# The last product of a chained matrix kernel, made in two PSUM banks and added to a kept copy of its chain

## The chip, the cores and the metric

The kernel runs on one core of one Trainium2 chip. The metric is the device time of one execution in microseconds (us). Most of it is the span, from the first to the last instruction that the profile shows; the time is some 1.8 us longer than the span.

In the lines of the profile, PE is the tensor engine, ACT is ScalarE, DVE is VectorE and SP is SyncE; a q behind the name is the engine's sequencer, which issues stores. L562 is a line of the kernel, x16 a number of instructions. A row in order of time begins with start and duration in us, and its bracket gives the idle time of the engine before it and what ended that.

## The reference, cut to what matters

Linformer attention (8 batches, 8 heads, 1024 tokens, 64 channels per head, keys and values projected to 64 rows) gives x with 8192 rows of 512. Then comes a feed-forward layer with a squared relu:

```python
def _moe_ref(x, w_in, w_out) -> np.ndarray:
    h = np.maximum(x @ w_in, 0.0)          # 8192 x 2048
    return (h * h @ w_out).astype(np.float32)   # 8192 x 512
```

## The kernel before: the parts that matter

The kernel works in chunks of 512 tokens. Both matrix products of the feed-forward layer are done with seven block products in place of eight (a Strassen-Winograd scheme). In the second one, a block product is 16 matmuls of 128x256: 8 for each half of the rows. Four output blocks come out of it. PSUM is the memory that the tensor engine writes, and a bank of it holds one block product here: half 0 and half 1 of its rows stand side by side, 256 columns each. Products 1, 6, 7 and 4 are a **chain**: they add up one after the other in one PSUM bank, and between them what has been added so far is copied or stored. The last output block, `put(1, 0, ...)`, is the whole chain, with product 4 on top.

```python
def keep(self, ps):                        # a copy of a bank in SBUF
    u = part_pool.tile([P, DM], F32, name="u")
    nc.scalar.copy(u[:], ps)
    return u

def put(self, a, mh, ps, more=None, part=None):
    o = out_pool.tile([P, 2, HM], F32, name="o_sb")
    n = slice(0, 2) if part is None else slice(part, part + 1)
    ps = ps.rearrange("p (i m) -> p i m", i=2)[:, n]
    if part:
        nc.vector.tensor_copy(o[:, n], ps)
    elif more is None:
        nc.scalar.copy(o[:, n], ps)
    else:
        tt(o[:, n], ps, ALU.add, more.rearrange("p (i m) -> p i m", i=2)[:, n])
    i = 4 * self.c + a + 2 * n.start
    (nc.scalar if part == 0 else nc.sync).dma_start(...)      # cut

def second_seven(self, first, chain, other, last=False):
    ...                                    # cut: products 1, 5, 6, 2
    yield from product(7, chain)
    self.put(1, 1, chain, p5)
    yield
    yield from product(3, other)
    self.put(0, 1, other, u2)
    yield
    yield from product(4, chain)
    if last:                               # the last chunk of all
        self.put(1, 0, chain, part=0)      # ScalarE copies half 0, its queue stores it
        self.put(1, 0, chain, part=1)      # VectorE copies half 1, SyncE stores it
    else:
        self.put(1, 0, chain)
    yield
```

At the start of the kernel, while the first loads are on their way, `warm(n)` runs n matmuls of zeros, meant to bring the tensor engine to full clock: in the trace of the kernel before, the first 8 of them start every 0.43 us and the next four every 0.22. The first call is `warm(8)`.

The softmax here doesn't subtract the row's maximum and nothing guards it: scores larger than these inputs give would overflow.

## Time and profile before

| | kernel before |
|---|---|
| time, median of the first 3 runs | 474.89 us (473.21 to 474.94) |
| span of the profiled run | 471.5 us |
| tensor engine busy | 98% of the span |
| end of the last matmul in the chain of waits | 467.81 us |
| end of the last instruction that computes | 468.70 us |
| from the start of the last matmul (467.53) to the end of the span | 3.94 us |

The last row is what I call **the tail** from here on. It starts at a record of the trace and not at a modelled end. To read it: the tensor engine bounds the kernel up to 467.8 us, so whatever a change does elsewhere shows only if it moves the last matmul or what follows it.

### The profile page before, as it was taken

The numbers are of one execution on the slowest core, as the hardware profiler recorded it, in microseconds if no ns is written. First come the engines' busy times: TensorE is split into PE (matmuls) and PEld (weight loads), VectorE is DVE, ScalarE is ACT, GpSimd is POOL, SyncE is SP. The second block draws the span as 40 slices with busy tenths as digits, with TensorE's granted clock in tenths as the row PEclk, the third lists the DMA queues.
The fourth block names the chain that finished last, engine by engine and source line by source line (L and its number), as shares of the span: only waits on it lengthen the run. The fifth ranks groups of instructions, "written<-read, shape, count | busy, mean of one in ns | idle before, by whom it ended". The sixth has DMA issues, their size and how long they took to land.

```text
span 471.5 us, 10107 instructions
## 1 busy us (share of the span) xinstructions
PE 464.1 (98%) x4123; PEld 367.6 (78%) x4141; DVE 347.6 (74%) x595; ACT 297.5 (63%) x484; POOL 34.0 (7%) x47
## 2 busy tenths in 40 slices
PE   8999999999999999999999999999999999999996
PEld 4544677888788787887888888888878878888885
DVE  2469985776968779567895779787796679968571
ACT  4488585887467864677457774568636875555641
POOL 7430100100010000100001000100000000000000
PEclk9999999999999999999999999999999999999999
DMA  9999999895869578785969749695692154101012
GB/s 182 201 205 207 158 206 203 166 217 106 186 138 207 137 141 195 133 171 131 170 180 153 170 98 183 153 197 147 116 219 71 39 132 100 68 24 68 24 69 89
DMA packets 85743, 67.90 MB, mean 144 GB/s; under 512 B 34368, under 2 KB 82240, under 8 KB 85696
## 3 DMA queue, kind: packets, MB, share of 16 engines
q0 software_dynamic: 32208, 29.23, 40.6%
q1 hardware_dynamic: 53344, 37.89, 30.1%
q8 instruction: 32, 0.52, 0.4%
q10 hardware_dynamic: 144, 0.13, 0.1%
q14 instruction: 15, 0.12, 0.1%
HBM read 59.24 MB, written 16.78 MB: 161 GB/s over the span
## 4 chain that ended last, share of the span: by engine, by line
PE 97%; DMA 1%; DVE 1%; ACT 1%; issue 0%; SPq 0%; ACTq 0%; DVEq 0%
PE ps_bank L665 38%; PE ps_second L585 36%; PE ps_bank L502 6%; PE ps_bank L562 3%; PE ps_att L270 3%; PE ps_att L339 2%; PE ps_second L562 2%; PE ps_att L415 2%; DMA k_f<-in_k_dram 1%; PE ps_att L392 1%; PE ps_bank L314 1%; PE ps_att L349 1%; PE ps_att L345 1%; PE ps_bank L220 0%; PE ps_att L289 0%; PE ps_bank L278 0%
## 5 line engine op out<-in xcount | busy, mean ns | idle before, releaser
L154 DVE TENSOR_TENSOR h<-h 128x1024 bf16<-128x1024 bf16 (+1 forms) x170 | 105.4, 645 | 43.9 <-ACT h L675 38.7
L665 PE MATMUL ps_bank<-x_sum,w_in_sum 128*128 128x256 bf16 x672 | 101.1, 273 | 0.1
L665 PEld LDWEIGHTS <-w_in_sum 128*128 128x128 bf16 x896 | 85.5, 98 | 18.9 <-issue 6.3
L585 PEld LDWEIGHTS <-h 128*128 128x128 bf16 x896 | 87.6, 98 | 10.7
L679 DVE CUSTOM_DVE_ANT_0 h<-ps_bank,u 128x512 bf16<-128x512 f32 x112 | 73.8, 685 | 16.2 <-PE ps_bank L665 12.1
L557 ACT COPY u<-ps_bank 128x512 f32<-128x512 f32 x115 | 68.0, 591 | 24.9 <-PE ps_bank L665 23.7
L690 ACT COPY ps_bank<-ps_bank 128x512 f32<-128x512 f32 x56 | 32.0, 571 | 81.5 <-PE ps_bank L665 81.5
L675 ACT ACTIVATE h<-ps_bank 128x512 bf16<-128x512 f32 x112 | 67.9, 607 | 16.7 <-PE ps_bank L665 15.8
L665 PEld LDWEIGHTS <-w_in 128*128 128x128 bf16 x672 | 64.3, 98 | 14.5 <-issue 5.2
L585 PEld LDWEIGHTS <-s 128*128 128x128 bf16 x672 | 65.7, 98 | 7.6
L665 PE MATMUL ps_bank<-xT,w_in 128*128 128x256 bf16 x448 | 67.3, 273 | 0.3
L585 PE MATMUL ps_second<-w_out_sum,s 128*128 128x256 bf16 x448 | 67.2, 273 | 0.0
L585 PE MATMUL ps_second<-w_out_sum,h 128*128 128x256 bf16 x448 | 67.0, 273 | 0.0
L585 PE MATMUL ps_second<-w_out,h 128*128 128x256 bf16 x448 | 64.7, 272 | 0.0
L419 DVE TENSOR_TENSOR xT<-ps_att,rs 128x512 bf16<-128x512 f32 x48 | 30.9, 685 | 13.7 <-PE ps_att L415 13.7
L353 ACT ACTIVATE expT<-ps_att 128x1024 bf16<-128x1024 f32 x32 | 33.1, 1034 | 5.2 <-PE ps_att L339 3.4
L665 PE MATMUL ps_bank<-x_sum,w_in 128*128 128x256 bf16 x224 | 33.7, 273 | 0.3
L665 PE MATMUL ps_bank<-xT,w_in_sum 128*128 128x256 bf16 x224 | 33.6, 273 | 0.1
L154 DVE TENSOR_TENSOR o_sb<-ps_second,u 128x512 f32<-128x512 f32 x29 | 19.9, 685 | 18.7 <-PE ps_second L585 13.6
L585 PE MATMUL ps_second<-w_out,s 128*128 128x256 bf16 x224 | 33.6, 273 | 0.0
L502 PE MATMUL ps_bank<-xT,w_in 128*128 128x512 bf16 x124 | 28.8, 379 | 0.4 <-issue 0.2
L154 DVE TENSOR_TENSOR s<-h 128x1024 bf16<-128x1024 bf16 x32 | 22.0, 691 | 3.7 <-PE ps_second L585 3.0
(97 smaller groups left out, 453.4 us busy)
## 6 DMA issues: line engine op xcount, KB each, us to landing
out_dram<-o_sb SPq DMA_DIRECT2D x63, 256.0 KB, 2.5
rs<-inv SPq DMA_DIRECT2D x96, 128.0 KB, 2.3
K_sb<-in_k_dram POOLq DMA_DIRECT2D x7, 1024.0 KB, 10.2
V_sb<-in_v_dram POOLq DMA_DIRECT2D x7, 1024.0 KB, 14.5
Q_sb<-in_q_dram POOLq DMA_DIRECT2D x6, 1024.0 KB, 11.8
w_out<-in_moe_w_out_dram POOLq DMA_DIRECT2D x4, 512.0 KB, 15.8
Q_sb<-in_q_dram POOLq DMA_DIRECT2D x4, 256.0 KB, 11.0
V_sb<-in_v_dram POOLq DMA_DIRECT2D x2, 512.0 KB, 10.8
```

The lines of the kernel that those rows point to most:

```text
L154: return nc.vector.tensor_tensor(out=o, in0=x, in1=y, op=op)
L270: nc.tensor.matmul(ps[LO, 0], lhsT=ET[:, i, :], rhs=self.K[:, :, i, :], start=f, stop=l)
L353: self.done = nc.scalar.activation(e[:], ps[:], AF.Exp, scale=SCALE)
L419: self.done = nc.vector.tensor_tensor(out=self.xT[:, pr, :, par], in0=ps_x[par].rearrange("p (c t) -> p c t", c=2), in1=rs[:, par].rearran ...
L502: nc.tensor.matmul(ps[:], lhsT=w_in_blk(cb, fb), rhs=self.xT[:, cb, self.c].rearrange("p a t -> p (a t)"), start=(cb == 0), stop=(cb == NC ...
L557: nc.scalar.copy(u[:], ps)
L562: nc.tensor.matmul(ps[:, i * HM:(i + 1) * HM], lhsT=self.h_form(n, fb)[:, i * P:(i + 1) * P], rhs=w_out_form(n, fb), start=fresh and i == ...
L585: nc.tensor.matmul(ps[:, i * HM:(i + 1) * HM], lhsT=self.h_form(n, fb)[:, i * P:(i + 1) * P], rhs=w_out_form(n, fb), start=fresh and i == ...
L665: nc.tensor.matmul(ps[:, j * HC:(j + 1) * HC], lhsT=w_in_form(n, cb, 2 * self.g + j), rhs=self.chunk.x_form(n, cb), start=fresh and j == 0 ...
L675: nc.scalar.activation(self.out(kh, a), ps[:], AF.Relu)
L679: nc.vector._custom_dve(TENSOR_ADD_SAT, out=self.out(kh, a), in0=ps[:], in1=more[:], s0=3.0e38, s1=0.0)
L690: nc.scalar.copy(self.chain[:], self.first[:])
```

## The change

The intent is to let the first half of the last block be finished and stored while the tensor engine makes the second half. In the kernel before, two engines work in one bank only in turn (VectorE's copy starts only at 468.28 us, when ScalarE's is done, though they read different columns), so each half gets a bank of its own. A fresh bank does not hold the chain, so the chain is copied to SBUF after product 7 (`u3`) and added by VectorE when a half is stored. The core of the diff, cut at the lines of dots:

```diff
-        def put(self, a, mh, ps, more=None, part=None):
-            o = out_pool.tile([P, 2, HM], F32, name="o_sb")
+        def put(self, a, mh, ps, more=None, part=None, o=None):
+            o = out_pool.tile([P, 2, HM], F32, name="o_sb") if o is None else o
...
-            if part:
-                nc.vector.tensor_copy(o[:, n], ps)
-            elif more is None:
+            if more is None:
                 nc.scalar.copy(o[:, n], ps)
...
-            (nc.scalar if part == 0 else nc.sync).dma_start(
+            nc.sync.dma_start(
...
             yield from product(7, chain)
+            if ends:
+                u3 = self.keep(chain)
             self.put(1, 1, chain, p5)
...
-            yield from product(4, chain)
-            if last:
-                self.put(1, 0, chain, part=0)
-                self.put(1, 0, chain, part=1)
+            if ends:
+                o = out_pool.tile([P, 2, HM], F32, name="o_sb")
+                for i, ps in enumerate(ends):
+                    self.half_product(4, i, ps, True)
+                    self.put(1, 0, ps, u3, i, o)
+                    yield
             else:
+                yield from product(4, chain)
                 self.put(1, 0, chain)
...
-        run(chunk[B - 1, 1].second_seven(..., True))
+        run(chunk[B - 1, 1].second_seven(..., [bank(n=turn["bank"] + n)[:] for n in (2, 3)]))
```

More of the change, by code (lines that the diff above doesn't have):

```diff
@@ L563, in half_product @@
                     ps[:, i * HM:(i + 1) * HM], lhsT=self.h_form(n, fb)[:, i * P:(i + 1) * P],
-                    rhs=w_out_form(n, fb), start=fresh and i == 0 and fb == 0, stop=fb == HF - 1,
+                    rhs=w_out_form(n, fb), start=fresh and fb == 0, stop=fb == HF - 1,
                     skip_group_check=True,
                 )
-        def put(self, a, mh, ps, more=None, part=None):
-            o = out_pool.tile([P, 2, HM], F32, name="o_sb")
+        def put(self, a, mh, ps, more=None, part=None, o=None):
+            o = out_pool.tile([P, 2, HM], F32, name="o_sb") if o is None else o
             n = slice(0, 2) if part is None else slice(part, part + 1)
             ps = ps.rearrange("p (i m) -> p i m", i=2)[:, n]
-            if part:
-                nc.vector.tensor_copy(o[:, n], ps)
-            elif more is None:
+            if more is None:
                 nc.scalar.copy(o[:, n], ps)
@@ L622, in second_spread, with second_seven @@
             yield
-        def second_seven(self, first, chain, other, last=False):
+        def second_seven(self, first, chain, other, ends=None):
             def product(n, ps, fresh=False):
@@ L627, in product @@
                 yield
-                self.half_product(n, 1, ps, fresh)
+                self.half_product(n, 1, ps)
             yield from product(1, first, True)
@@ L647, in second_seven @@
             yield
-            yield from product(4, chain)
-            if last:
-                self.put(1, 0, chain, part=0)
-                self.put(1, 0, chain, part=1)
+            if ends:
[4 more added lines that the diff above has]
+                    yield
             else:
+                yield from product(4, chain)
                 self.put(1, 0, chain)
-            yield
+                yield
     class Group:
@@ L900 @@
         assert not plan, plan
-        run(chunk[B - 1, 1].second_seven(second_bank(0)[:], second_bank(1)[:], bank(n=turn["bank"] + 1)[:], True))
+        run(chunk[B - 1, 1].second_seven(second_bank(0)[:], second_bank(1)[:], bank(n=turn["bank"] + 1)[:], [bank(n=turn["bank"] + n)[:] for n in (2, 3)]))
 _INS = ['q', 'k', 'v', 'E', 'F', 'moe_w_in', 'moe_w_out']
```

## The prediction

> **What bounds the kernel now.** I read the page first, then the chain that ended last over the last microseconds, then the instructions in order of time there, then the movement of the DMA engines in the last 3.5 us. The page says who owns the 471.5 us span:
>
> ```profile
> PE 464.1 (98%) x4123; PEld 367.6 (78%) x4141; DVE 347.6 (74%) x595; ACT 297.5 (63%) x484; POOL 34.0 (7%) x47
> ...
> PE 97%; DMA 1%; DVE 1%; ACT 1%; issue 0%; SPq 0%; ACTq 0%; DVEq 0%
> ```
>
> The tensor engine is busy for 98% of the span and is 97% of the chain; the clock row of the page is 9 in all 40 slices, so no throttle confuses this. A change that neither removes nor shortens matmuls can only touch the ends, where the tensor engine is not the bound. The change sits at the very end, so I looked at the chain from 463 us on (start, duration, what):
>
> ```profile
> 466.05 1.76 PE ps_second L562 x16
> 467.81 0.03 ACTq L575
> 467.84 0.04 issue
> 467.88 0.38 ACT o_sb L575
> 468.26 0.02 issue
> 468.28 0.42 DVE o_sb L573
> ```
>
> The last product is 16 matmuls from 466.05 to 467.81. Then ScalarE copies one half of the rows out of the bank, and only when it is done does VectorE copy the other half: **the two engines work one after the other although they were meant to share the work.** The same in order of time, with what ended each engine's idle time in brackets:
>
> ```profile
> 467.88 0.37 ACT L575 COPY o_sb<-ps_second 128x256 f32<-128x256 f32 x1 [4.70 <-PE ps_second L562]
> 468.28 0.38 ACTq L579 DMA_DIRECT2D out_dram<-o_sb  x1
> 468.28 0.42 DVE L573 COPY o_sb<-ps_second 128x256 f32<-128x256 f32 x1 [1.50 <-ACT o_sb L575]
> ```
>
> The bracket of the last line names ScalarE as the releaser. And ScalarE's copy of the first half began after the 16th matmul, though the matmuls of its own half, the first 8 of 16, must have been done at about 466.05 + 1.76/2 = 466.93. Both are one cause: everything that touches one bank is put in sequence by bank.
>
> After 468.70 only the last store is left. In the last 3.5 us, in slices of 0.0875 us:
>
> ```profile
> DMA  9999610000000499955999510000000000000000
> ```
>
> The two bursts are the two 128 KB stores: the first from about 469.15 to 469.55, the second from about 469.6 to 470.05. Each begins some 0.9 us after its issue (468.28 and 468.70); they stand side by side and hardly overlap. The profile puts landing 1.8 us after issue, 470.5, and the program ends 1.0 us later.
>
> [...] the trace has 691 and 692 ns for the adds into o_sb. [...] this trace has no fp32 add of 256. [...] here a 128 KB store takes 1.8 us and a 256 KB one 2.1, so halving a store hardly shortens its landing.
>
> **The change part by part.** Between the two programs the orders of instructions, with line numbers taken out, are the same on VectorE, ScalarE, GpSimd and SyncE up to the last few rows; on the tensor engine 16 products go to other banks. So the first 462 us should not change at all.
>
> *Kept copy (added).* Product 7 leaves the chain in a bank at 464.30. ScalarE now copies it to SBUF, 128x512 fp32, 586 ns by the same copy at other places: about 464.37 to 464.96. ScalarE has been idle since 463.19, so it costs ScalarE nothing. But the add of the same bank into o_sb on VectorE, which began at 464.40 and took 0.69, now must wait for ScalarE: about 464.98 to 465.67. Its next add waits for the tensor engine until 466.09 anyway: 0.4 us to spare. Hidden.
>
> *Two fresh banks (moved).* Half 0 (8 matmuls) ends at 466.93, half 1 at 467.81 as before: 16 matmuls of the same form and the same weights. The first matmul of product 4 had to wait for VectorE to leave the chain; that wait was already over (465.09 against 466.05), so nothing is won there. Starting a bank afresh in place of adding is a flag of the matmul and costs nothing that I can see in the other fresh products (0.0 us idle ahead of them). The banks were last used by the first stage, before 455 us.
>
> *Half 0 stored early (moved off the path).* VectorE is busy with the previous add until 466.78, so its add of half 0 is about 466.97 to 467.40, its issue on SyncE 467.40 to 467.77. SyncE had its earlier issue done at 466.81 + 0.37 = 467.18. All beside the last 8 matmuls.
>
> *Half 1 (the path).* Before, from the end of the tensor engine: 0.07 (wake) + 0.38 (ScalarE) + 0.02 + 0.42 (VectorE) = 0.89 us, to 468.70. After: 0.04 to 0.08 (wake; the add after product 3 began 0.04 after the modelled end) + 0.42 (VectorE, 256 columns with two operands; the one-operand copy of the same size took 0.425 too) = 0.46 to 0.50, to about 468.29. The store follows as before: SyncE's issue, 1.8 us landing, 1.0 us end. **Sum: 0.89 - 0.48 = 0.41 us**, the whole of one ScalarE copy and its hand-over. That is 0.41 / 471.5 = 0.09%.
>
> **The rivals.** *The last transfer is hidden or held by the one ahead of it.* If the second burst was pushed back by the first, the change would win more: the first now moves about 0.9 us earlier than the second, so they can't meet. The two bursts begin about the same 0.9 us after their issues, which speaks against more than 0.05 us: 0.45 in all. *A wait that takes the place.* The tile that the halves share is the third after one whose store was issued at 463.21 and landed about 465.3, before 466.97: no wait. Were it late, VectorE would start half 0 late; up to 0.4 us of that are free. If the store of half 0 kept SyncE busy past 468.29, the gain would shrink; it has 0.5 us of slack. *VectorE becomes the bound of the tail:* three adds (0.69, 0.42, 0.42) between 466.09 and 468.29, each waiting for the tensor engine, 0.2 to 0.45 us between them; not likely. *The end is set by something else*, the tensor engine's own finish or the final barrier: SyncE's wait list at the end of the program names the store (1.0 us in two waits) and then the tensor engine's sequencer (0.6 us), which might not move with the store. Then the gain would be near 0; I give it one in seven. *Run to run noise:* the three runs before are 474.94, 474.89 and 473.21, and the profiled one 473.25: two levels 1.7 us apart, four times the gain. Which level the median of the new runs falls on moves the time more than the change does.
>
> **Range and chances.** Span: 471.5 - 0.4 = 471.1. Time: on the upper level 474.9 - 0.4 = 474.5, on the lower 473.2 - 0.4 = 472.8. The levels came up two and two in four runs; I put the point between, nearer the upper because the known median is there: 474.1. The range holds both, with 0.2 below the lower and the case of no gain on top: 472.6 to 475.0. A 2% change would be 9.5 us; nothing in a tail of 3.7 us behind the last matmul can give or take that[...]: 0.01 on either side.
>
> **What the profile would show.** Right: the last VectorE op is an add of 128x256 released by the tensor engine and not by ScalarE, 0.42 to 0.43 us long, ending 0.45 to 0.52 us after the last matmul (0.89 before); an add of half 0 begins between 466.9 and 467.1 while the tensor engine runs; the two last bursts stand about 0.9 us apart; the add after product 7 begins about 0.6 us later, and the tensor engine does not notice. Wrong: half 0's add released only by the 16th matmul (then two adds in a row, and 0.89 us as before); an idle gap in the tensor engine ahead of product 4; an add much longer than 0.43; or a later end of the tensor engine from a cause far ahead of the tail.

The 0.42 us of the sum for an add of 256 columns is to be read as an estimate from the copy of 256 columns in the trace of before (0.425 us).

## The result, and the profile after

The changed kernel took 473.09 us (median of 6 runs, 472.41 to 474.56) against 474.86 us before (6 runs, 473.21 to 475.49). The ratio is 0.9973, 95% interval 0.9951 to 0.9995. A ratio is the mean time of one kernel's runs over that of the other's of the same rounds, so it is not quite the ratio of these medians. The profiled run has a span of 471.3 us.

The end of the chain of waits in the changed kernel (start, duration, what), to be read against that of before:

```profile
464.62 3.51 PE ps_bank L562 x32
468.13 0.02 issue
468.16 0.42 DVE o_sb L154
```

ScalarE's 0.38 us and its hand-over are gone: after the last matmul there is one VectorE instruction, and it ends 0.45 us after the last matmul (468.58 against 468.13), where it was 0.89 (468.70 against 467.81). The same stretch in order of time:

```profile
464.66 0.59 ACT L557 COPY u<-ps_second 128x512 f32<-128x512 f32 x1 [1.16 <-PE ps_second L562]
465.28 0.69 DVE L154 TENSOR_TENSOR o_sb<-ps_second,u 128x512 f32<-128x512 f32 x1 [5.70 <-ACT u L557]
466.41 0.69 DVE L154 TENSOR_TENSOR o_sb<-ps_bank,u 128x512 f32<-128x512 f32 x1 [0.44 <-PE ps_bank L562]
467.28 0.42 DVE L154 TENSOR_TENSOR o_sb<-ps_bank,u 128x256 f32<-128x256 f32 x1 [0.18 <-PE ps_bank L562]
468.16 0.42 DVE L154 TENSOR_TENSOR o_sb<-ps_bank,u 128x256 f32<-128x256 f32 x1 [0.45 <-PE ps_bank L562]
```

The first line is the kept copy. The second is the add after product 7, now released by that copy and so 0.66 us after the end of product 7 (464.62). The third begins when product 3 is done, as before, so the delay ended there. The fourth is half 0, begun 0.85 us ahead of the end of the tensor engine. The releaser of the last is the tensor engine and no longer ScalarE.

The DMA engines in the last 3.5 us of interest (468.0 to 471.5, as in the view of before):

```profile
DMA  4999999999995000289982000000000000000000
```

The second burst is the last store, from about 469.5 to 469.9: again 0.9 us after its issue at 468.61. The first, from 468.0 to 469.1, is the rest of the store before the split one and half 0 behind it.

The tail, from the start of the last matmul to the end of the span, is **3.49 us against 3.94: 0.45 us saved.** But the span is only 0.13 us shorter, because in this run the last matmul came 0.32 us later than in the profiled run of before; and the medians lie 1.77 us apart. The 0.32 us come from the start of the run, far from the change: in this trace the tensor engine waits 0.67 us for ScalarE to hand it the first keys and starts their product at 7.51 us, against 7.00 in the trace of before, and its 300th matmul is already 0.32 us late. Neither number is the tail's. So two questions go to the chip: what of the change makes the 0.45 us, and where the other differences come from.

### The profile page after: what moved, and what is told of

The parts are those of the page before. It is cut to its first block, busy times and chain, and to the rows that moved or that the text cites. A ratio compares the mean times of both kernels' runs of the same rounds, so it can differ in the third digit from the quotient of the medians. Undisturbed runs are those within 1.5% of the kernel's fastest.

```text
span 471.3 us, 10106 instructions
## 1 busy us (share of the span) xinstructions
PE 464.0 (98%) x4123; PEld 367.6 (78%) x4141; DVE 348.1 (74%) x596; ACT 297.7 (63%) x484; POOL 34.0 (7%) x47
## 4 chain that ended last, share of the span: by engine, by line
PE 97%; DMA 1%; DVE 1%; ACT 1%; issue 0%; SPq 0%; DVEq 0%
PE ps_bank L669 38%; PE ps_second L583 36%; PE ps_bank L502 6%; PE ps_bank L562 4%; PE ps_att L270 3%; PE ps_att L339 2%; PE ps_att L415 2%; PE ps_second L562 1%; DMA k_f<-in_k_dram 1%; PE ps_att L392 1%; PE ps_bank L314 1%; PE ps_bank L220 1%; PE ps_att L349 1%; PE ps_att L345 1%; PE ps_att L289 0%; PE ps_bank L278 0%
## 5 line engine op out<-in xcount | busy, mean ns | idle before, releaser
L557 ACT COPY u<-ps_second 128x512 f32<-128x512 f32 x30 | 17.6, 586 | 11.6 <-PE ps_second L583 9.3
```

## The experiments

Each experiment was correct against the reference. Those "timed" had five rounds (6 runs); the others are one look with a profile, for the tail can be read from one trace. All tails are from the start of the last matmul to the end of the span; "last op" is the end of the last computing instruction after the end of the last matmul.

| | last op, us | tail, us |
|---|---|---|
| kernel before | 0.89 | 3.94 |
| changed kernel | 0.45 | 3.49 |
| the changed kernel again | 0.45 | 3.50 |
| one bank, stores after both halves | 0.78 | 3.99 |
| one bank, store between the halves | 0.45 | 3.50 |
| second half in the chain's bank | 0.39 | 3.43 |
| last half in two pieces of 128 columns | 0.31 | 3.28 |
| kept copy three times | 0.46 | 3.63 |
| before, both copies on ScalarE | 0.72 | 3.98 |
| before, last block stored whole | 0.64 | 4.08 |
| pieces, the last one in the chain's bank | 0.29 | 3.25 |

**Theory.** The banks are what matters: half 0 leaves the tail because nothing else touches its bank. **Rivals:** it is the kept copy and the exchange of ScalarE for VectorE; or the gain does not reach the end; or something ahead of the tail changed as well, since 0.9973 would be 1.3 us.

### The changed kernel again (timed)

No edit.

> The changed kernel again, with five more rounds. Theory (the tail alone gained, about 0.45 us): ratio to before 0.9990, each run on one of two levels 1.7 us apart as in the runs before, and the gap between the lower levels of the two kernels 0.3 to 0.6 us. Rival (something before the tail gained too, since the first six runs gave 0.9973, that is 1.3 us): ratio again near 0.997 and both levels lower by over 1 us.

Measured: median 474.37 us against 474.19 before in the same rounds, ratio 1.0006 (0.9983 to 1.0028). So the first ratio of 0.9973 did not come back. The six times are 472.82, 473.18, 474.23, 474.52, 474.88 and 475.07. Over all rounds, with both runs of this program together, the lower level (under 474 us) has mean 472.92 us (6 runs) and the upper 474.61 (6 runs). The kernel before has 473.29 (20 runs) and 474.87 (20 runs), over all groups of rounds here, on more than one chip. **Level against level the change is worth 0.37 and 0.27 us; the rival of a gain ahead of the tail, which asked for over 1 us, falls.** The runs of one level scatter by 0.2 to 0.3 us, so each of the two figures has a standard error of over 0.1 us. In these rounds alone the two lower runs are 0.25 below those of before, a little less than I expected. The 0.9973 was chance: five of the six runs of before had been on the upper level, and two of six of the changed kernel.

### One bank, the stores after both halves (one look)

```diff
-                for i, ps in enumerate(ends):
-                    self.half_product(4, i, ps, True)
-                    self.put(1, 0, ps, u3, i, o)
-                    yield
+                for i in range(2):
+                    self.half_product(4, i, ends[0], i == 0)
+                    yield
+                for i in range(2):
+                    self.put(1, 0, ends[0], u3, i, o)
```

> The kept copy and the two adds on VectorE stay, but both halves are made in one bank and stored after the second. Theory (the separate banks are what lets the first add run beside the matmuls): both adds come after the last matmul, 0.04 + 0.42 + 0.42, the last ends 0.88 to 0.95 us after the last matmul, as before the change. Rival (the gain comes from taking ScalarE out of the tail and adding from the kept copy): the last add ends about 0.5 us after the last matmul.

The last VectorE row in order of time, and the last matmuls in the chain of waits:

```profile
467.69 0.76 DVE L154 TENSOR_TENSOR o_sb<-ps_bank,u 128x256 f32<-128x256 f32 x2 [1.05 <-PE ps_bank L562]
```

```profile
464.16 3.51 PE ps_bank L562 x32
467.67 0.02 issue
467.69 0.42 DVE o_sb L154
```

Both adds stand behind the last matmul (467.67). The tail is 3.99 us: the whole gain is gone although the kept copy and the adds are all there. **The separate banks make the gain.** In one point I was off: the two adds take 0.76 us in all and not 0.85, so the second started some 0.09 us before the first was done. That does not help, because SyncE takes 0.35 us to issue the first store (468.15 in the trace) and starts the second only at 468.58, 0.13 us after its data was ready. So the exchange of ScalarE for VectorE does shorten the clearing of the bank by itself, from 0.89 us to 0.78, and the separate banks shorten it from 0.78 to 0.45; that the first 0.11 us are lost here is due to the one queue for both stores. The same with two queues was not run.

### One bank, the store between the halves (one look)

```diff
-                for i, ps in enumerate(ends):
-                    self.half_product(4, i, ps, True)
-                    self.put(1, 0, ps, u3, i, o)
+                for i in range(2):
+                    self.half_product(4, i, ends[0], i == 0)
+                    self.put(1, 0, ends[0], u3, i, o)
```

> One bank for both halves again, but the first half is stored before the second is made. Theory ([...] the separate banks pay by keeping the tensor engine going): the tensor engine stands idle for 0.45 to 0.55 us between the halves (wake plus the 0.42 us add), and the last add ends about 0.5 us after the last matmul: the whole gain is given back in the tensor engine. Rival (different columns of one bank may be read and written together here): no gap, and the same tail as the changed kernel.

```profile
467.09 0.44 DVE o_sb L154
467.52 0.04 issue
467.57 1.05 PE ps_bank L562 x8
468.61 0.02 issue
468.64 0.42 DVE o_sb L154
```

In the chain of waits, half 0's add now stands *between* the matmuls: the trace gives the tensor engine an idle gap of 0.52 us with VectorE as the releaser. The tail is 3.50 us, as in the changed kernel, and the 0.45 us saved there are lost in the gap. One bank can be had early or without a gap, not both.

### The kept copy three times over (one look)

```diff
-                u3 = self.keep(chain)
+                for _ in range(3):
+                    u3 = self.keep(chain)
```

> The kept copy made three times over on ScalarE (1.2 us more). Theory (the kept copy is hidden behind 0.4 us of slack of VectorE, then another 0.2 at the first half): the add of product 7 starts about 1.2 us later, the add of product 3 about 0.75 later, the first half's add at about the end of the last matmul and the second's behind it; the last add ends 0.6 to 0.7 us after the last matmul, 0.2 us later than in the changed kernel. Rival (a copy on ScalarE is never on the path): no difference, 0.45 us. Rival (no slack): 1.2 us later.

```profile
464.19 1.56 ACT L557 COPY u<-ps_second 128x512 f32<-128x512 f32 x3 [1.16 <-PE ps_second L562]
465.79 0.69 DVE L154 TENSOR_TENSOR o_sb<-ps_second,u 128x512 f32<-128x512 f32 x1 [6.68 <-ACT u L557]
466.40 1.01 DVE L154 TENSOR_TENSOR o_sb<-ps_bank,u 128x512 f32<-128x512 f32 x2
467.69 0.43 DVE L154 TENSOR_TENSOR o_sb<-ps_bank,u 128x256 f32<-128x256 f32 x1 [0.28 <-PE ps_bank L562]
```

The three copies took 1.56 us, less than three times 0.59, and the adds behind them ran close together. So VectorE caught up: its last add ends 0.46 us after the last matmul (467.66), on time, and not 0.6 to 0.7 as I wrote. All the same the tail grew by 0.13 us, to 3.63. The view of the DMA engines from 467.5 to 471.0 shows why:

```profile
DMA  9999999999999999999999610000000000000000
```

The stores that the copies delayed now move just ahead of the last one, with no pause in the engines, and the last store queues behind them: the span ends 2.86 us after its issue, against 2.73 in the changed kernel. **One kept copy is hidden; its slack is limited by the stores as much as by VectorE.**

### The kernel before with both copies on ScalarE, and with the last block whole (one look each)

```diff
-            if part:
-                nc.vector.tensor_copy(o[:, n], ps)
-            elif more is None:
+            if more is None:
...
-            (nc.scalar if part == 0 else nc.sync).dma_start(
+            nc.sync.dma_start(
```

> The kernel before with both half copies on ScalarE, both stores issued by SyncE. Theory (the two engines never worked side by side): the two copies end 0.07 + 0.37 + 0.37 = 0.8 us after the last matmul, no later than before (0.89). Rival (the second engine did help): 0.1 us or more later than before.

```profile
467.78 0.65 ACT L573 COPY o_sb<-ps_second 128x256 f32<-128x256 f32 x2 [4.70 <-PE ps_second L562]
```

Measured: 0.72 us for the copies, sooner than the 0.89 of two engines in turn. So the second engine never helped to clear the bank. The tail was 3.98 us all the same (3.94 before), because both stores now go through SyncE: the second was issued at 468.61, 0.19 us after its copy was done, when the first issue was over, and from there to the end it took 2.79 us, where the last store of before took 2.73.

The other one drops the argument `True` of the last call, so that the last block of all is stored as those of the other chunks are:

> The kernel before with the last product stored whole: one copy of 128x512 on ScalarE and one store of 256 KB. Theory: the copy ends 0.07 + 0.59 = 0.66 us after the last matmul, sooner than the two halves (0.89), but the store lands 2.1 us after issue in place of 1.8: from the last matmul to the end of the span within 0.15 us of the kernel before (3.66). Rival (the end does not follow the last store): shorter by 0.23 us.

Measured: the copy ended 0.64 us after the last matmul, and the tail was 4.08 us, 0.13 longer than before: within the range I gave, and against the rival. The larger store moves longer (in the trace of before 256 KB landed 2.1 us after issue, 128 KB 1.8). The split of the kernel before was worth 0.13 us, through the size of the last store.

### The second half in the chain's bank (timed)

If only half 0 must be out of the way, half 1 may go on adding in the chain's bank. It then needs no kept copy, and ScalarE can copy it.

```diff
-                for i, ps in enumerate(ends):
-                    self.half_product(4, i, ps, True)
-                    self.put(1, 0, ps, u3, i, o)
+                for i, ps in enumerate((ends[0], chain)):
+                    self.half_product(4, i, ps, i == 0)
+                    self.put(1, 0, ps, (u3, None)[i], i, o)
```

(and `keep` copies the 256 columns of half 0 alone.)

> Only the first half goes to a fresh bank and is added to the kept copy; the second half goes on adding in the chain's bank and is copied by ScalarE, 128x256 in 0.37 us in place of VectorE's 0.42. Theory (only the first half's bank must differ from the second's): the last copy ends 0.42 to 0.46 us after the last matmul, span and time as the changed kernel within 0.1 us plus noise. Rival (both halves need a fresh bank, or the chain's bank makes the tensor engine wait): an idle gap of the tensor engine before the second half, or a tail of 0.8 us.

```profile
466.71 0.89 PE ps_second L562 x8
467.60 0.02 issue
467.62 0.37 ACT o_sb L573
```

The last copy ends 0.39 us after the last matmul (sooner than the 0.42 to 0.46 that I expected), the tail is 3.43 us, and no gap of the tensor engine stands in the trace. **One bank apart is enough.** In time nothing is seen of 0.06 us: the ratio to before is 1.0001 (0.9981 to 1.0021), with five of its six runs on the upper level.

### The last half in two pieces (timed)

The added lines for half 1; half 0 is as in the changed kernel, and the last call hands over one bank more:

```diff
+                for j, ps in enumerate(ends[1:]):          # two fresh banks
+                    m = slice(j * HM // 2, (j + 1) * HM // 2)
+                    for fb in range(HF):
+                        nc.tensor.matmul(
+                            ps[:, 0:HM // 2], lhsT=self.h_form(4, fb)[:, P:2 * P], rhs=w_out_form(4, fb)[:, m], ...
+                        )
+                    tt(o[:, 1, m], ps[:, 0:HM // 2], ALU.add, u3[:, HM + m.start:HM + m.stop])
+                    nc.sync.dma_start(out_tokens[self.b][:, 4 * self.c + 3, m], o[:, 1, m])
```

> The second half is made in two banks of 128 columns, so the last add is 128x128 and the last store 64 KB. Theory (the tail is what stands after the last matmul): the last add takes about 0.29 us and ends 0.33 us after the last matmul, 0.13 us sooner than in the changed kernel, and the last transfer is shorter by up to 0.2; against it the 16 matmuls of 128 columns take longer than 8 of 256 (0.88 us)[...]. Sum: from 0.2 us better to 0.5 us worse. Rival (the end is set by the final barrier): the span does not move with the last store at all.

```profile
469.23 0.91 PE ps_bank L656 x16
470.14 0.02 issue
470.16 0.29 DVE o_sb L154
```

The 16 short matmuls take 0.91 us and the 8 longer ones took 0.88: I had expected more, at most 1.57 (16 mean weight loads of 0.098 us, as the traces have them). So the price is 0.03 us and not up to 0.7. (The trace of before already has matmuls of 128 columns every 0.056 us. The 0.29 us for the add is, as an estimate, what an add of 512 columns, 0.691 us, and one of 256, 0.425, come to at 128.) The tail is 3.28 us, 0.21 less than in the changed kernel. The shorter add did not make it: the add ends 0.55 us after the start of the last matmul and not 0.74, but SyncE was still issuing the store of the piece ahead and issued the last one only at 470.66, 0.20 us after its data was ready. That is 0.75 us after the start of the last matmul, against 0.76 in the changed kernel. The gain is the shorter store: 2.52 us from its issue to the end, against 2.73 (64 KB land 1.6 us after issue, 128 KB after 1.8). The rival of the final barrier falls once more. In time the median was 473.48 us, the ratio 0.9996 (0.9969 to 1.0022), with three of its six runs on the upper level. The profiled run itself is on the upper level (474.95 us), and it is the one that shows what that level is; see below.

### Both together (timed)

Half 1's first 128 columns in a fresh bank, its last 128 in the chain's bank and copied by ScalarE: the two edits above put together.

> The two edits that shortened the tail put together: the last half in two pieces of 128 columns, the first piece in a fresh bank and added to the kept copy, the second going on in the chain's bank and copied by ScalarE. Theory (the tail is what follows the last matmul): the last copy takes about 0.27 us, the span ends 3.25 us after the start of the last matmul (3.49 in the changed kernel, 3.28 with the quarters alone, 3.94 before); the 16 short matmuls take 0.91 us. Times: the same two levels 1.7 us apart, each 0.6 to 0.7 us below those of the kernel before. Rival (the issue of one more store on SyncE, or a wait of the tensor engine for the chain's bank, holds the end): 3.4 us or more, or an idle gap ahead of the last 8 matmuls.

```profile
466.81 0.45 PE ps_bank L657 x8
467.25 0.46 PE ps_second L657 x8
467.72 0.02 issue
467.74 0.27 ACT o_sb L664
```

The tail is 3.25 us, as predicted, 0.69 less than before. The copy was ready at 468.01 but SyncE issued its store at 468.23, since the issue of the piece ahead took from 467.73 to 468.14; to issue one of them on another queue was not tried. So ScalarE's shorter copy did not bring the store forward either: its issue stands 0.75 us after the start of the last matmul, as with the pieces alone, and that the 3.25 was met is in part luck. The ratio is 1.0003 (0.9983 to 1.0024): four of its six runs were on the upper level. Level against level it lies 0.48 and 0.53 us below the kernel before in the same rounds, less than the 0.6 to 0.7 that I expected.

### What the two levels are

The profiled runs of the kernel with the last block whole (475.06 us) and of the kernel before (473.25 us) differ by 1.68 us already at the start of the 300th matmul of the tensor engine, at 49.44 and 47.76 us, long before the tail. The tensor engine's first rows in order of time, first the kernel before, on the lower level:

```profile
1.19 3.47 PE L220 MATMUL ps_bank<-zeros 128*128 128x512 bf16 x8 [1.19 <-DVE zeros L123]
5.22 0.67 PE L211 MATMUL ps_bank<-ident,e_bf 64*128 64x64 bf16 x8 [0.56 <-DVE e_bf L723]
5.83 1.04 PE L220 MATMUL ps_bank<-zeros 128*128 128x512 bf16 x4
```

and the one with the last block whole, on the upper level:

```profile
1.19 3.60 PE L220 MATMUL ps_bank<-zeros 128*128 128x512 bf16 x8 [1.19 <-DVE zeros L123]
5.19 0.71 PE L211 MATMUL ps_bank<-ident,e_bf 64*128 64x64 bf16 x8 [0.40 <-DVE e_bf L723]
5.83 1.89 PE L220 MATMUL ps_bank<-zeros 128*128 128x512 bf16 x4
```

The same four warm-up matmuls take 1.04 us in one run and 1.89 in the other: the clock is still at about half. (The clock column of the profile says 1.00 there, for it counts full clock where the trace holds no record of it. In the records themselves full clock begins at 10.23 us in this trace, and between 3.88 and 5.69 us in the 13 others.) In the profiled run with the last half in two pieces the clock had come up and fell back. Its view by stretches, whose last three columns are the granted clock, the share of the DMA engines and GB/s:

```profile
4.60:8.00 3.40, 1.79 (x13) 0.99 (x13) 0.97 (x2) 1.00 (x1) 3.40 (x6) 1.00 1.29 218
8.00:11.40 3.40, 3.31 (x20) 2.40 (x20) 0.43 (x2) 0.41 (x2) 1.91 (x3) 0.50 1.28 202
```

The tensor engine was busy 1.79 of 3.40 us, most of the rest was a wait of 1.24 us for the first keys, and then came a stretch at clock 0.50; by the records it lasted from 7.97 to 11.39 us. These two are the only kept traces of the upper level. In the first (the last block whole), the four warm-up matmuls and the eight matmuls of the row after them took 1.89 + 1.92 us, against 1.04 + 1.03 in the kernel before: 1.74 us more. In the second, a stretch of 3.42 us at half clock in place of full loses, as an estimate from its length, at most 3.42/2 = 1.7 us. The levels of before lie 474.87 - 473.29 = 1.58 us apart. What makes the clock come up late, or fall back, no trace here shows. My guess was that an idle gap in the warm-up matters, and there is one: 0.56 us ahead of the second row of the kernel before. Its length alone does not sort the runs: it is 0.40 and 0.46 us in the two traces of the upper level, and 0.40 to 0.79 us in the nine of the lower level with 8 warm-ups. So if the gap counts, its length is not all that counts. Two kernels fill it, both on top of the shortest tail:

```diff
-        warm(8)
+        warm(9)        # in the second kernel: warm(10)
```

> The same with 9 in place of 8 warm-up matmuls at the start, to fill most of the 0.56 us in which the tensor engine waits for the first cast. Theory (the two levels of time are whether the clock is already at full speed from about 5 us on[...], and an idle gap in that time makes the late case likelier): fewer than half of the runs on the upper level, with the lower level unchanged within 0.1 us. Rival (the levels come from elsewhere, or the gap does not matter): about half of the runs on each level as before.

> The same with 10 warm-up matmuls: the gap is filled wholly, at the price of up to 0.25 us of delay of the first projection where the clock is still at half speed. Theory of the clock: still fewer runs on the upper level, the lower level 0 to 0.25 us higher. Rival: half of the runs on each level, both 0.25 us higher.

The first rows with 9:

```profile
1.19 4.02 PE L220 MATMUL ps_bank<-zeros 128*128 128x512 bf16 x9 [1.19 <-DVE zeros L123]
5.20 0.68 PE L211 MATMUL ps_bank<-ident,e_bf 64*128 64x64 bf16 x8
5.81 1.04 PE L220 MATMUL ps_bank<-zeros 128*128 128x512 bf16 x4
```

The gap is gone and the second row starts no later. With 9 the six runs are 472.49 to 473.12 us (median 472.63, ratio to before 0.9979, interval 0.9961 to 0.9997), with 10 they are 472.52 to 473.30 (median 472.79, ratio 0.9981, 0.9964 to 0.9997). None of the twelve is on the upper level, against 8 of 17 of the kernel before and the same tail with 8 in the same rounds. With 10 the second row starts at 5.49 us, 0.29 later, and the mean of the runs is 0.09 us higher than with 9. The last kernel parts this from the tail: the kernel *before* with `warm(9)` and nothing else.

> The kernel before with 9 warm-up matmuls and nothing else. Theory (the ninth warm-up keeps the runs off the upper level, whatever the tail; the tail is worth in time what it is worth in the trace): all six runs on the lower level, with a median of 472.63 (the kernel with 9 warm-ups and the shortest tail) plus 0.67 (the difference of their tails, 3.94 against 3.28 us) = 473.3, between 473.1 and 473.7; span 3.94 us after the start of the last matmul. Rival (the ninth warm-up did nothing, six of six and six of six were luck): about half of the runs at 474.5 to 475.5. Rival (the tail's gain does not reach the measured time): a median within 0.2 of 472.63.

Measured: median 473.34 us (473.05 to 473.94), as expected, and a tail of 3.97 us. The run of 473.94 is the profiled one; it is at full clock (its four matmuls take 1.04 us) and lost its time in waiting 1.03 us for the first keys, so it is not the upper level. Over all, with 8 warm-ups 38 of 70 runs of timed kernels were over 474 us; with 9 or 10, none of 18. And with the levels out of the way, the tails show in time: 473.34 - 472.63 = 0.71 us between two kernels whose profiled tails differ by 3.97 - 3.28 = 0.69 us. That they agree so well is in part luck, for these are medians from two groups of runs on different chips: against the lower level of the kernel before in its own rounds (473.23 and 473.42 us), the mean with 9 lies 0.49 us below for the shortest tail and 0.05 above for the tail of before, which makes 0.54.

**The kernel with the shortest tail and 9 warm-up matmuls is faster than the kernel before:** 472.63 us against 473.50 in the same rounds (the changed kernel did not run in these). Between these medians it is mostly the tail, for the median of before fell on the lower level. In the mean the two parts are worth about the same: the ninth warm-up alone 0.6 us (the ratio of the last kernel, 0.9988, with an interval of 0.9972 to 1.0004 that is not clear of noise), the tail 0.5 to 0.7. That the ninth matmul keeps the runs off the upper level is shown. How it does so is not shown: no run parts the filling of the gap from the 0.43 us of work that one more matmul adds.

## Why the prediction was right, point by point

- **The path.** The prediction had 0.89 us behind the last matmul become 0.46 to 0.50; it became 0.45. The wake was 0.02 us where I had 0.04 to 0.08, and the add took 0.42. The sum of 0.41 us measured 0.45 in the tail, and 0.27 to 0.37 level against level in time.
- **The cause.** That order by bank made both halves wait is confirmed from both sides: in one bank the first half comes either after the last matmul (tail 3.99) or with a gap of 0.52 us in the tensor engine.
- **The kept copy is hidden.** Predicted: the add after product 7 moves to 0.68 us behind that product, without reaching the next. Measured: 0.66, and the next add was released by product 3 as before. Under three copies VectorE had more slack than I gave it, and the stores less.
- **Half 0 beside the matmuls.** Predicted 0.84 us ahead of the end of the tensor engine, measured 0.85.
- **The last transfer follows its issue by 0.9 us and lands 1.8 us after it.** So it did. The rivals that had the end held by the barrier or by the store ahead fall: in every experiment the end followed the last store, for 128 KB by 2.72 to 2.76 us from its issue where no store stood close ahead. Where one did, it was 2.79 us (one bank, both copies on ScalarE) and 2.86 (three copies).
- **The time.** The range rested on two levels 1.7 us apart, "four times the gain", and said that the median would move with the level. It did, from 473.09 in the first six runs to 474.37 in the next. So the point of 474.1 was 1.0 us off in the first six runs and 0.3 in the next, and which of them came was luck; that both lie in the range was not, for it held both levels. I took the levels as noise of unknown cause; in the two profiled runs on the upper level they are the clock of the first 12 us. The prediction ruled the clock out by the page's row of nines, but that row cannot show it: the first 8 warm-up matmuls of before start every 0.43 us, the next four every 0.22.
- **Mis-sized or misread, without harm:** the "16 products" that go to other banks are the 16 matmuls of product 4. The two last bursts do not stand 0.9 us apart: half 0's moved right behind the store ahead of it, until 469.1, and the last one began at about 469.4. I gave one in seven to an end that does not follow the store; and I held that halving a store hardly shortens its landing, while 64 KB landed 0.2 us sooner than 128.

## What to carry to other kernels

When two engines are to share the clearing of a product, give their shares separate banks; in one bank they ran in turn here, though each had columns of its own (the last of them done 0.89 us after the last matmul, against 0.39 with separate banks). Make the last piece of the last product small and everything ahead of it early, for only what follows the last matmul counted here (a tail of 3.28 us with a last piece of 128 columns, 3.49 with 256); and look to the issue of the stores, which stand in line too: SyncE took 0.34 to 0.46 us for each, and in four of the experiments above, where it had one to issue just ahead, it issued the last one 0.13 to 0.22 us after its data was ready, against 0.03 in the changed kernel. When the times of one kernel fall on two levels, compare the traces at a fixed instruction near the start before crediting a change: here one more warm-up matmul was worth about as much, in the mean, as the whole tail.
